# Four-tap filter of k as two passes in two 64-column tiles, with the moving operand stacked from two shifts

## Chip, cores, metric

The kernel runs on one core of a Trainium2 chip. The metric is the device time of one execution in microseconds. Each version was run several times. Every run is fast or slow (slow: over 1.5% above the fastest run of the same kernel), and only fast runs are compared. One execution of each version was traced, and all stage times below come from these traces.

## The reference, cut to what matters

The network is a gated long convolution followed by a two-layer MLP, on 2048 tokens of 512 channels. The change touches the first step only: a causal filter of `k` over four tokens, one set of four weights for each channel, multiplied by `v`.

```python
ks = 4
k_pad = jnp.pad(k, ((0, 0), (ks - 1, 0), (0, 0)))
k_shift = jnp.zeros_like(k)
for t in range(ks):
    k_shift = k_shift + k_pad[:, t:t + S, :] * shift_k[:, ks - 1 - t][None, None, :]
kv = k_shift * v
# ... kv is convolved with ssm_k over all 2048 tokens (by FFT), plus kv * ssm_D,
#     gated by layernorm(q), added to q; then layernorm, relu MLP, residual
```

## The kernel before

`k` arrives transposed, channels on partitions, in four chunks of 512 tokens. A unit is one chunk of 128 channels, so there are 16 units. TensorE computes a unit with four accumulating matmuls against diagonal weights, each reading `k` one token earlier. VectorE then multiplies the result in PSUM by `v`.

```python
def taps(u):
    c, rg = divmod(u, DC)
    ps = psum.tile([P, CH], F32, tag="ps", name="pkv")
    for j in range(KS):
        nc.tensor.matmul(out=ps[:], lhsT=wdiag[:, rg, j, :],
                         rhs=kT[:, rg, CH * c + 16 - j:CH * c + CH + 16 - j],
                         start=(j == 0), stop=(j == KS - 1))
    return u, ps
# times_v(u, ps): VectorE, kvx[...] = ps * vT[...]
```

The units of chunks 1 to 3 are interleaved with `group_k`, the first stage of the long filter's transform: 64 small matmuls, whose four results ScalarE (three) and VectorE (one) copy out. All these tiles take turns in eight PSUM banks.

```python
for gb in range(8):
    for u in ((4, 5), (6,), (7, 8), (9,), (10, 11), (12,), (13, 14), (15,))[gb]:
        times_v(*taps(u))
    group_k(gb)
for pq in halves:          # dre, dim: eight small GpSimd products that read dsc ("dm_f" in the trace)
    ...
# ... to_rows: TensorE transposes kv; needs the product of the last unit
pl.pop("early")            # the memory of dsc, d0, kfl, kvx and others is given back,
pl.pop("vp")
slotB = pl.push("slotB")   # and kf is laid over it
kf = slotB.tile([P, 2, 256, 32], F32R, tag="B", name="kf")
```

GpSimd negates a sine table, `cn` ("c2n" in the trace), in eight slices. Before the change it does so early.

## Time and profile before

| what | before |
|---|---|
| time, median of four fast runs (220.4 over the first three) | 220.3 us |
| traced span | 218.7 us |
| loop of taps and groups (to the transposes of kv) | ends at 37.0 us |
| second transform stage starts to use products (first `psy` matmul) | 67.4 us |
| first matmul of the MLP | 125.6 us |

The last three rows are milestones: each is the start of the first matmul that writes a given tile. If a change alters only the loop, the later milestones move by the same amount.

### The profile page before, as it was taken

Reading aid. Unit: us, or ns where it says so; the run is one execution under the profiler, and the core shown is the slowest. Engines: PE = TensorE matmul, PEld = TensorE weight load, DVE = VectorE, ACT = ScalarE, POOL = GpSimd, SP = SyncE. Lnnn points to the kernel's source line nnn. Section 1 sums busy time; section 2 is a strip of 40 time slices with the busy share of each in tenths; the row PEclk is TensorE's granted clock in tenths of the full one; section 3 lists DMA queues with packets and bytes.
Section 4 is the critical chain, followed back from the end, with each engine's and each line's share of the span. In section 5 each row is a group of like instructions: output and inputs, shape, how many; then the busy total and the mean of one; then the engine's idle time right before and its main releaser. Section 6 shows DMA issues by size and latency. Waiting matters only on the chain.

```text
span 218.7 us, 7281 instructions
## 1 busy us (share of the span) xinstructions
PE 202.8 (93%) x3103; PEld 139.4 (64%) x3122; DVE 148.2 (68%) x304; ACT 127.7 (58%) x242; POOL 65.9 (30%) x99
## 2 busy tenths in 40 slices
PE   7879889999979999989987899999999999999993
PEld 2276446999968999879965587444444444444442
DVE  7978868899979999957968779742973257130032
ACT  2587858788867888858966699003740066206500
POOL 6059920000029999969200120210021002000000
PEclk9969999999999999999999999999999999999999
DMA  6999960000000000059970000332022110421012
GB/s 96 383 224 191 142 136 7 3 4 3 6 3 0 1 0 3 1 134 216 305 252 3 6 0 3 42 77 55 24 52 63 42 47 0 96 57 42 0 42 54
DMA packets 30383, 15.40 MB, mean 70 GB/s; under 512 B 25520, under 2 KB 29072, under 8 KB 30224
## 3 DMA queue, kind: packets, MB, share of 16 engines
q1 hardware_dynamic: 29520, 14.76, 29.9%
q8 instruction: 24, 0.39, 0.8%
q10 hardware_dynamic: 832, 0.20, 0.4%
q14 instruction: 7, 0.06, 0.1%
HBM read 7.08 MB, written 2.10 MB: 42 GB/s over the span
## 4 chain that ended last, share of the span: by engine, by line
PE 83%; ACT 6%; DMA 4%; issue 2%; DVE 2%; SPq 1%; ACTq 0%
PE ps2m L568 17%; PE ps1m L556 16%; PE pz L482 8%; PE psi L449 7%; PE psy L375 7%; PE pst L217 5%; PE ps L244 4%; PE pkv L271 4%; PE ps2k L259 4%; DMA pre<-in_A_ssm_k_dram 4%; PE ps2k L261 3%; PE u L259 3%; PE u L261 3%; ACT ecore L143 1%; SPq L121 1%
## 5 line engine op out<-in xcount | busy, mean ns | idle before, releaser
L556 PE MATMUL ps1m<-hlnT,w 128*128 128x512 bf16 (+3 forms) x219 | 39.5, 336 | 0.3
L558 ACT ACTIVATE h1T<-ps1m 128x512 bf16<-128x512 f32 (+3 forms) x55 | 27.4, 514 | 21.2 <-PE ps1m L556 20.3
L568 PE MATMUL ps2m<-w,h1T 128*128 128x512 bf16 (+3 forms) x177 | 38.9, 366 | 0.7 <-issue 0.3
L570 DVE TENSOR_TENSOR o<-ps2m,xh 128x512 bf16<-128x512 f32 (+1 forms) x17 | 11.1, 659 | 38.1 <-PE ps2m L568 37.6
L556 PEld LDWEIGHTS <-w 128*128 128x128 bf16 (+1 forms) x220 | 21.7, 100 | 17.6 <-issue 1.4
L568 PEld LDWEIGHTS <-h1T 128*128 128x128 bf16 (+1 forms) x187 | 17.6, 98 | 21.2 <-issue 3.1
L365 DVE TENSOR_TENSOR t<-u,kf 128x704 fp32r<-128x704 f32 x32 | 26.7, 887 | 2.9 <-ACT usb L361 2.6
L365 POOL TENSOR_TENSOR t<-usb,kf 128x320 fp32r<-128x320 f32 x32 | 28.1, 922 | 1.4 <-ACT usb L361 1.0
L493 ACT CAST zt<-pz 128x512 bf16<-128x512 f32 x16 | 8.4, 592 | 29.2 <-PE pz L482 29.2
L482 PE MATMUL pz<-bp,ecore 32*32 32x128 f32 x1024 | 22.5, 384 | 2.3 <-issue 1.4
L231 ACT CAST a<-ps 128x512 fp32r<-128x512 f32 (+1 forms) x42 | 21.2, 575 | 4.3 <-PE ps L244 4.2
L502 POOL TENSOR_SCALAR rstd<-mv 128x4 f32<-128x4 f32 (+1 forms) x7 | 1.6, 232 | 70.3 <-DVE mv L509 70.3
L482 PEld LDWEIGHTS pz<-bp,ecore 32*32 32x32 f32 x1024 | 14.2, 103 | 9.4 <-issue 5.4
L231 ACT CAST kf<-psy 128x512 fp32r<-128x512 f32 x30 | 17.4, 640 | 1.7 <-PE psy L375 0.2
L233 DVE CAST a<-ps 128x512 fp32r<-128x512 f32 (+1 forms) x26 | 16.1, 647 | 3.1 <-PE ps L244 2.9
L507 DVE BATCH_NORM_STATS2 st<-xh 128x6 f32<-128x512 bf16 x28 | 17.4, 680 | 0.0
L449 PE MATMUL psi<-dre,kf 128*128 128x256 f32 x64 | 15.5, 284 | 0.9 <-ACT kf L231 0.9
L375 PE MATMUL psy<-t,ipos 128*128 128x512 f32 x48 | 15.8, 391 | 0.0
L271 PE MATMUL pkv<-kT,wdiag 128*128 128x512 bf16 x56 | 14.8, 380 | 0.8 <-DMA kT<-in_A_k_dram 0.3
L449 PE MATMUL psi<-dim,kf 128*128 128x256 f32 x64 | 15.4, 283 | 0.0
L209 POOL TENSOR_SCALAR c2n<-c2s 128x512 fp32r<-128x512 f32 x8 | 11.9, 1559 | 8.9 <-ACT c2s L177 8.9
L449 PEld LDWEIGHTS psi<-dre,kf 128*128 128x128 f32 x64 | 12.3, 192 | 1.3 <-ACT kf L231 1.3
(115 smaller groups left out, 377.0 us busy)
## 6 DMA issues: line engine op xcount, KB each, us to landing
pre<-in_A_ssm_k_dram SPq DMA_DIRECT2D x1, 2048.0 KB, 8.7
out_dram<-o SPq DMA_DIRECT2D x58, 32.0 KB, 1.6
xh<-in_A_q_dram SPq DMA_DIRECT2D x4, 384.0 KB, 6.8
w<-in_B_w_dram SPq DMA_DIRECT2D x1, 1376.0 KB, 12.7
w<-in_B_w_dram SPq DMA_DIRECT2D x1, 1280.0 KB, 15.8
xh<-in_A_q_dram SPq DMA_DIRECT2D x4, 128.0 KB, 2.8
hlnT<-hln SPq DMA_TRANSPOSE x12, 2.4
w<-in_B_w_dram SPq DMA_DIRECT2D x1, 96.0 KB, 15.4
```

What stands on the lines that cost most here:

```text
L231: nc.scalar.copy(out=o, in_=i)
L233: nc.vector.tensor_copy(out=o, in_=i)
L259: nc.tensor.matmul(out=ps[:, kk, :], lhsT=w_re[:, k1, :], rhs=a_in(col(k1, 0)), start=True, stop=False, skip_group_check=True)
L271: nc.tensor.matmul(out=ps[:], lhsT=wdiag[:, rg, j, :], rhs=kT[:, rg, CH * c + 16 - j:CH * c + CH + 16 - j], start=(j == 0), stop=(j == KS ...
L365: eng.tensor_tensor(out=t[:, :, j, :], in0=in0.unsqueeze(1).to_broadcast([P, 2, n, 2]), in1=kfr[:, :, j, ks], op=ALU.mult)
L375: nc.tensor.matmul(out=psy[:], lhsT=m_[:], rhs=t_.rearrange("p j k -> p (j k)"), start=first, stop=not first)
L449: nc.tensor.matmul(out=ps[:, i, :], lhsT=kf[:, c, 4 * m:4 * m + 4, :].rearrange("p r k -> p (r k)"), rhs=d[:].rearrange("p a b -> p (a b)" ...
L482: nc.tensor.matmul(out=pz[32 * a:32 * a + 32, r4, l4, :], lhsT=ecore[rows, rho, n2, :], rhs=rhs, start=(rho == 0), stop=(rho == 1), tile_p ...
L507: nc.vector.bn_stats(out=st[:, t % 4, :], in_=xh[:, t, :])
L556: nc.tensor.matmul(out=ps1[:fsz, :], lhsT=w1[:, c, fc * P:fc * P + fsz], rhs=hlnTs[sc][:, c, part], start=(c == 0), stop=(c == DC - 1))
L558: nc.scalar.activation(out=h1s[sc][:fsz, fc, part], in_=ps1[:fsz, :], func=ACT.Relu)
L568: nc.tensor.matmul(out=ps2[:], lhsT=h1s[sc][:ksz, fc, i * P:(i + 1) * P], rhs=w2[:ksz, fc, ds], start=(fc == 0), stop=(fc == NFC - 1))
```

## The change

The intent is to halve TensorE's work on chunks 1 to 3. A diagonal weight matrix of 128 x 128 uses one row for each column. The change instead lets 128 rows hold 64 channels twice, once as they are and once two tokens later, so that one pass does two taps for 64 channels. The two halves of the channels sit in two tiles of 64 columns, which can run at the same time. The price is three VectorE copies for each chunk, which build the stacked operand. In the code, `lo` and `hi` are partitions 0 to 63 and 64 to 127.

```diff
     def taps(u):
         ...
-        for j in range(KS):
-            nc.tensor.matmul(out=ps[:], lhsT=wdiag[:, rg, j, :], rhs=kT[:, rg, ...],
-                             start=(j == 0), stop=(j == KS - 1))
+        if c == 0:
+            ...                       # as before
+        else:
+            for p in range(2):
+                for hf, (src, o) in enumerate(((kAs[c], 2), (kTs[c], 16))):
+                    nc.tensor.matmul(out=ps[halves[hf], :], lhsT=wd2[:, rg, hf, p, :],
+                                     rhs=src[:, rg, o - p:o - p + CH],
+                                     start=(p == 0), stop=(p == 1),
+                                     tile_position=(0, 64 * hf), skip_group_check=True)
+    def pair_up(c):
+        kA = kAs[c] = kvp.tile([P, DC, CH + 2], BF16, tag="kA", name="kA", bufs=2)
+        kc = kTs[c]
+        nc.vector.tensor_copy(out=kA[lo, :, :], in_=kc[lo, :, 14:16 + CH])
+        nc.vector.tensor_copy(out=kA[hi, :, :], in_=kc[lo, :, 12:14 + CH])
+        nc.vector.tensor_copy(out=kc[lo, :, 14:16 + CH], in_=kc[hi, :, 12:14 + CH])
 ...
+    pair_up(1)                        # after the transposes of the long filter
     for gb in range(8):
-        for u in ((4, 5), (6,), (7, 8), (9,), (10, 11), (12,), (13, 14), (15,))[gb]:
+        group_k(gb)
+        if gb == 2:
+            pair_up(2)
+        if gb == 4:
+            pair_up(3)
+        for u in ((4, 5), (6, 7), (8, 9), (10, 11), (12,), (13, 14), (15,), ())[gb]:
             times_v(*taps(u))
-        group_k(gb)
+        if gb == 4:                   # GpSimd's negated table, moved here from before the loop;
+            ...                       # its first write reads a result of pair_up(3), so that it waits
     for pq in halves:
         ...                           # dre and dim: unchanged text, now behind that table on GpSimd
 # ... also: k loaded into four tiles with 16 tokens of overlap; wq, wd2: the new weights, on VectorE
```

More of the change, by code (lines that the diff above doesn't have):

```diff
@@ L104 @@
     vTs = [vp.tile([P, DC, CH], BF16, name=f"vT{c}") for c in range(4)]
-    kT = kvp.tile([P, DC, 16 + S], BF16, name="kT")
+    kTs = [kvp.tile([P, DC, 16 + CH], BF16, name=f"kT{c}") for c in range(4)]
+    kAs = {}
+    wq = kvp.tile([P, DC, 2, 2], BF16, name="wq")
     wdiag = kvp.tile([P, DC, KS, P], BF16, name="wdiag")
@@ L113 @@
         nc.tensor.matmul(out=warm[:], lhsT=wz[:, 0:P], rhs=wz[:], start=True, stop=True)
-    nc.vector.memset(kT[:, :, 0:16], 0.0)
+    nc.vector.memset(kTs[0][:, :, 0:16], 0.0)
     for c, src in ((0, "k"), (0, "s"), (0, "v"), (1, "k"), (1, "v"), (2, "k"), (2, "v"), (3, "k"), (3, "v")):
@@ L120 @@
         elif src == "k":
-            nc.sync.dma_start_transpose(out=kT[:, :, 16 + CH * c:16 + CH * c + CH], in_=k_d[ts, :])
+            if c == 0:
+                nc.sync.dma_start_transpose(out=kTs[0][:, :, 16:16 + CH], in_=k_d[ts, :])
+            else:
+                nc.sync.dma_start_transpose(out=kTs[c][:], in_=k_d[CH * c - 16:CH * c + CH, :])
         else:
@@ L168 @@
                                 in1=wsh[:, rg, :].unsqueeze(2).to_broadcast([P, KS, P]), op=ALU.mult)
+    id64 = early.tile([P, 64], BF16, name="id64")
+    nc.vector.tensor_tensor(out=id64[:], in0=ident[:, 0:64], in1=ident[:, 64:128], op=ALU.add)
+    wd2 = kvp.tile([P, DC, 2, 2, 64], BF16, name="wd2")
     cc = wp.tile([P, 32, P], F32R, name="c2c")
@@ L204 @@
     table(cc, r2[:], (0,))
-    dtab = consts.tile([P, 8, DC, 8], BF16, name="dtab")
-    for h in range(8):
-        hs = slice(4 * h, 4 * h + 4)
-        nc.gpsimd.tensor_single_scalar(out=cn[:, hs, :], in_=cs[:, hs, :].bitcast(F32), scalar=-1.0, op=ALU.mult)
-        if h == 0:
-            nc.gpsimd.tensor_copy(out=dtab[:], in_=d0[:].rearrange("p r (o g) -> p o r g", g=8))
+    for row in range(2):
+        for hf in range(2):
+            j0 = 0 if row == hf else 2
+            nc.vector.tensor_copy(out=wq[halves[row], :, hf, :], in_=wsh[halves[hf], :, j0:j0 + 2])
+    nc.vector.tensor_tensor(out=wd2[:].rearrange("p r h j i -> p (r h j) i"),
+                            in0=id64[:].unsqueeze(1).to_broadcast([P, 4 * DC, 64]),
+                            in1=wq[:].rearrange("p r h j -> p (r h j)").unsqueeze(2).to_broadcast([P, 4 * DC, 64]),
+                            op=ALU.mult)
     def to_rows(cols, q, fl, eng):
@@ L269, in taps @@
         ps = psum.tile([P, CH], F32, tag="ps", name="pkv")
-        for j in range(KS):
-            nc.tensor.matmul(out=ps[:], lhsT=wdiag[:, rg, j, :], rhs=kT[:, rg, CH * c + 16 - j:CH * c + CH + 16 - j],
-                             start=(j == 0), stop=(j == KS - 1))
-        return u, ps
+        if c == 0:
+            for j in range(KS):
+                nc.tensor.matmul(out=ps[:], lhsT=wdiag[:, rg, j, :], rhs=kTs[0][:, rg, 16 - j:16 - j + CH],
+                                 start=(j == 0), stop=(j == KS - 1))
+        else:
+            for p in range(2):
+                for hf, (src, o) in enumerate(((kAs[c], 2), (kTs[c], 16))):
+                    nc.tensor.matmul(out=ps[halves[hf], :], lhsT=wd2[:, rg, hf, p, :], rhs=src[:, rg, o - p:o - p + CH],
+                                     start=(p == 0), stop=(p == 1), tile_position=(0, 64 * hf), skip_group_check=True)
+        return u, ps
+    def pair_up(c):
[4 more added lines that the diff above has]
+        nc.vector.tensor_copy(out=kc[lo, :, 14:16 + CH], in_=kc[hi, :, 12:14 + CH])
     def times_v(u, ps):
@@ L306 @@
     for gb in range(8):
-        for u in ((4, 5), (6,), (7, 8), (9,), (10, 11), (12,), (13, 14), (15,))[gb]:
-            times_v(*taps(u))
-        group_k(gb)
+        group_k(gb)
[4 more added lines that the diff above has]
+        for u in ((4, 5), (6, 7), (8, 9), (10, 11), (12,), (13, 14), (15,), ())[gb]:
+            times_v(*taps(u))
+        if gb == 4:
+            dtab = consts.tile([P, 8, DC, 8], BF16, name="dtab")
+            nc.gpsimd.tensor_copy(out=dtab[lo, 0, 0, 0:1], in_=kTs[3][lo, 0, 14:15])
+            for h in range(8):
+                hs = slice(4 * h, 4 * h + 4)
+                nc.gpsimd.tensor_single_scalar(out=cn[:, hs, :], in_=cs[:, hs, :].bitcast(F32), scalar=-1.0, op=ALU.mult)
+                if h == 0:
+                    nc.gpsimd.tensor_copy(out=dtab[:], in_=d0[:].rearrange("p r (o g) -> p o r g", g=8))
     for pq in halves:
```

## The prediction

> **What bounds the kernel now.** I read the page's first two parts, then the chain of waits, to learn in which stage the changed instructions lie; then the busy time by stretch for that stage; then VectorE's own timeline there, because the change puts new work on that engine. The page says that TensorE is the engine to look at and that its clock dips only once, early:
>
> ```profile
> span 218.7 us, 7281 instructions
> PE 202.8 (93%) x3103; PEld 139.4 (64%) x3122; DVE 148.2 (68%) x304; ACT 127.7 (58%) x242; POOL 65.9 (30%) x99
> PEclk9969999999999999999999999999999999999999
> ```
>
> The share over the whole span is an average, so the stage decides. The chain of waits in order of time (start, duration, what; cut to 18 to 42 us) shows one unbroken alternation of tap matmuls (line L271) and first-stage matmuls of k (L244), all on TensorE, with two stretches of "issue":
>
> ```profile
> 22.39 0.66 PE ps L244 x61
> 23.04 0.32 PE pkv L271
> 23.42 1.46 PE pkv L271 x6
> 24.88 0.61 PE ps L244 x64
> ...
> 26.91 0.62 issue
> ...
> 31.63 0.73 issue
> ...
> 36.98 3.77 PE pst L217 x64
> ```
>
> So from 19 to 37 us TensorE sets the pace, and the taps carry it. The busy times by stretch (us; PE, PEld, DVE, ACT, POOL, granted clock, DMA share, GB/s) are the important view:
>
> ```profile
> 12.00:18.70 6.70, 6.41 (x65) 6.41 (x66) 5.49 (x10) 4.50 (x4) 5.27 (x5) 0.75 1.23 234
> 18.70:37.00 18.30, 16.12 (x554) 8.67 (x560) 13.85 (x22) 13.94 (x25) 10.17 (x15) 1.00 0.73 113
> 37.00:41.00 4.00, 4.00 (x68) 4.00 (x69) 3.86 (x7) 3.58 (x7) 0.00 (x0) 1.00 0.00 0
> ```
>
> In the middle row TensorE has 16.1 of 18.3 us, but VectorE and ScalarE are close behind with 13.9 each. If TensorE gets faster, the stage can shrink by some 4 us at most before another engine is full, and VectorE is the one that gets new work. Its timeline there (start, duration, idle before in brackets):
>
> ```profile
> 17.14 2.48 DVE L221 TENSOR_SCALAR kfl<-pst 128x512 int32<-128x512 int32 x4
> 20.39 1.29 DVE L278 TENSOR_TENSOR kvx<-pkv,vT 128x512 bf16<-128x512 f32 x2 [0.77 <-DMA vT<-in_A_v_dram]
> 27.97 0.69 DVE L233 CAST a<-ps 128x512 fp32r<-128x512 f32 x1 [0.78 <-PE ps L244]
> 32.09 0.69 DVE L278 TENSOR_TENSOR kvx<-pkv,vT 128x512 bf16<-128x512 f32 x1 [0.97 <-DMA vT<-in_A_v_dram]
> 36.23 0.69 DVE L278 TENSOR_TENSOR kvx<-pkv,vT 128x512 bf16<-128x512 f32 x1 [0.20 <-PE pkv L271]
> 37.66 3.97 DVE L221 TENSOR_SCALAR xfl<-pst 128x512 int32<-128x512 int32 x6
> ```
>
> The multiplication by v of the last tap unit ends at 36.92 us, and 0.06 us later the transposes of kv start on TensorE (36.98). From there on TensorE is busy to the end, so the time of the whole kernel moves with the end of that one VectorE instruction. That is the quantity I predict.
>
> **What the Trainium skill says.** "TensorEngine Tiling (Array Packing)", section Tiling Modes, says that tiles execute weight loads and matmuls independently and in parallel, and that changing the mode drains the engine. The trace before agrees on the first: the 256 matmuls per half of L244, in four row tiles, come four in some 0.03 us. The number of mode changes stays about the same, since taps (128 rows) and L244 (32 rows) already differ. "VectorE: DVE Perf Modes", section on the perf-mode tier table, gives 693 ns for a bf16 copy of 2048 elements within SBUF, its fastest mode; no such copy is in the trace before. "SBUF — State Buffer", section "SBUF: two separate sides", says that such a VectorE copy and a GpSimd instruction lock each other out for a whole instruction; the change moves the negated sine table (GpSimd) behind the last copy, so I expect no clash. "TensorE: Matmul & The Clock Gate", Part 1, says that TensorE falls to half clock after about a 3.4 us window of little work. The trace has the case: idle from about 10.2 to 12.3 us, then clock 0.50 to 16 us.
>
> **The change part by part.**
> TensorE: chunks 1 to 3 have 12 tap units of 4 matmuls over 512 columns. A unit pair takes from 22.98 to 24.81 us, 1.83 us, so a unit costs about 0.9 us and a matmul about 0.21. Now a unit is two passes of two concurrent tiles, about 0.43 us. That removes 12 x 0.43 = 5.1 us from TensorE. What is left there: 12 x 0.43 + 8 x 0.65 (L244) + 1.4 of issue = 11.8 us.
> ScalarE: 24 casts at 0.52 us pitch (three take 1.56) = 12.5 us, unchanged.
> VectorE, old work: 8 casts and 12 multiplications; back to back such instructions come every 0.61 us (four of L221 in 2.48 us, each 0.69). 20 x 0.61 = 12.2 us.
> VectorE, new work: nine copies, three for each chunk, of 64 partitions x 4 x 514 = 2056 bf16. From the row of L46 (64 elements 196 ns, 2048 elements 1228 ns, int32, so 0.52 ns an element and 163 ns fixed) and half of that slope for bf16, one costs 163 + 2056 x 0.26 = 698 ns, in accord with the skill's 693. With some overlap of neighbours I take 0.68 each: 2.05 us per chunk and 6.15 in all. There are also four small weight copies (about 0.15 each), the new weight table of 1024 elements (L167 takes 688 ns for 512, at one element a cycle another 512 are 0.53: 1.22 us) and the 64-column identity (0.2).
>
> Where it lies. The weight table comes after the cosine turns end at 12.24 us. VectorE is idle there for 1.03 us until the first transposes arrive, so about 0.9 of its 2.0 us delay the evictions of kfl: their end moves from 19.62 to about 20.5. TensorE's first-stage group 0 needs all of them, and starts at about the old time (20.6 against 20.42), because the taps that stood before it are now behind it. Then VectorE, in program order, has three copies, group 0's cast, two multiplications and so on, to the last multiplication: 6.15 + 19 x 0.61 = 17.7 us. Twice, for chunks 2 and 3, the next VectorE instruction is the multiplication whose taps wait for the copies just made: two passes, their latency and the signal back, about 0.7 us of idle each. For chunk 1 a cast lies between.
> Sum: 20.5 + 17.7 + 1.4 = 39.6 us, against 36.92 before: +2.7 us. VectorE takes TensorE's place as the bound, and the 5.1 us gained become TensorE waiting.
> GpSimd: the table is 8 x 1.48 us pitch (7 in 10.34) and starts near 35.5 us; its first slice is there at 37, the first use is after 43, and a slice is used every 2.7 us. It stays off the path. The transposing loads grow by 3% (528 rows for 512); k's chunk 3 is issued at 22.3 and lands some 5.6 us later, well before its copies at about 33.
>
> **The rivals.**
> (a) VectorE absorbs the copies. For it: VectorE idles about 4.3 us between 19.62 and 36.92 (17.3 us less 20 instructions at about 0.65). Against it: the new work is 6.15 in the loop plus 0.9 before it. At a pitch of 0.55 for a copy, without the two waits, the end is about 37.1 us: no change, 220.5. A gain of over 4.4 us needs VectorE's work to vanish, which I cannot see.
> (b) The copies do not run in the fastest mode, because of their 64 partitions, four rows or crossing of partitions. At half rate a copy is 163 + 1070 = 1.23 us, nine are 11.1: another 4.9 us, about 228. Everything is even and aligned, so I hold it unlikely.
> (c) The clock. While copies for a chunk run, TensorE has about 2.8 us without work, more than the idle stretch that cost it its clock at 13 us. One or two cold windows of 3.4 us double some 2 us of work each: +1 to +3 us, above all if one falls into the 3.8 us of transposes. I add 0.3 to the middle for it and widen the range upwards.
> (d) The two column tiles do not overlap. TensorE then has 17 us as before beside VectorE's 19: still VectorE-bound, with waits of 1.1 in place of 0.7 us, about 224.
>
> **Range and chances.** 220.4 + 2.7 + 0.3 = 223.4; rival (a) pulls down, so I take 223.1. From (a) without waits (220.5) to (c) with two cold windows (226) is my 8 in 10. Slower by over 2% means above 224.8: it needs (b), (c) or (d) on top, 0.21. Faster by over 2% means below 216.0: 0.03. The rest, 0.76, is within 2%.
>
> **What would show it right or wrong.** Right: VectorE over 90% busy from about 20 to 40 us; nine copies near 0.7 us; TensorE's matmuls there waiting for VectorE; idle VectorE of about 0.7 us after the copies of chunks 2 and 3; the transposes of kv starting near 39.6 us and everything after them the same length. Wrong: transposes starting before 37 us (copies cheaper or hidden), copies at 1.2 us, or a granted clock of 0.5 in slices between 20 and 45 us.

## More of the kernel before

GpSimd matters later, so here are two lines of its timeline in the kernel before (start, duration, instruction). They show that the table is done at 25.6 us and that the last of the small products that read `dm_f` is done at 29.1 us:

```profile
15.27 10.34 POOL L209 TENSOR_SCALAR c2n<-c2s 128x512 fp32r<-128x512 f32 x7
...
28.32 0.80 POOL L312 TENSOR_SCALAR dim<-dm_f 64x64 fp32r<-64x64 f32 x2
```

## The result, and the profile after

The change made the kernel slower. Its four fast runs took 230.46 to 232.91 us, median 231.77, against 220.31 for the kernel before. The ratio is 1.0506, with a 95% interval of 1.0427 to 1.0585. A ratio here is the mean time of one kernel's fast runs over that of the other's of the same rounds, so it is not quite the ratio of the quoted medians. The traced run of the changed kernel is the slowest of its four (232.91 us), so the two traced spans lie 12.4 us apart where the medians lie 11.5 apart.

The head of the page of the changed kernel. In the last line, each digit is the granted clock of one of 40 slices in tenths; slices 4 to 7 (17 to 40 us) and 10 (52 to 58 us) have fallen from 9, and slice 3 was low before too:

```profile
span 231.1 us, 7304 instructions
PE 206.5 (89%) x3111; PEld 141.3 (61%) x3122; DVE 155.6 (67%) x319; ACT 127.5 (55%) x242; POOL 66.0 (29%) x100
PEclk9977677997999999999999999999999999999999
```

The busy times by stretch, with the same columns as in the prediction (us; PE, PEld, DVE, ACT, POOL, clock, DMA share, GB/s):

```profile
18.70:37.00 18.30, 12.24 (x355) 6.37 (x353) 14.95 (x24) 10.67 (x18) 0.00 (x0) 0.72 0.79 116
37.00:41.00 4.00, 3.04 (x72) 1.49 (x74) 2.52 (x4) 0.71 (x3) 2.53 (x4) 0.61 0.02 4
49.00:51.00 2.00, 1.28 (x70) 1.03 (x68) 0.00 (x0) 0.00 (x0) 2.00 (x3) 1.00 0.03 8
51.00:53.00 2.00, 0.00 (x0) 0.00 (x0) 0.00 (x0) 0.00 (x0) 1.81 (x7) 1.00 0.00 0
```

Two things stand out. From 18.7 to 37 us no engine is full (VectorE, the fullest, has 14.95 of 18.3 us), although the stage is longer than before, and the clock is 0.72 instead of 1.00. From 51 to 53 us only GpSimd works.

The milestones put sizes on them:

| milestone | before | after | moved by |
|---|---|---|---|
| transposes of kv start | 37.0 | 43.9 | 6.9 |
| first `psy` matmul | 67.4 | 80.0 | 12.6, so 5.7 more |
| first matmul of the MLP | 125.6 | 138.0 | 12.4 |
| end of the span | 218.7 | 231.1 | 12.4 |

So there are two losses: 6.9 us in the loop, and 5.7 us between the transposes and the first product. Nothing after that changed.

VectorE's timeline of the changed kernel (start, duration, idle time before in brackets) answers the one in the prediction:

```profile
17.69 2.48 DVE L233 TENSOR_SCALAR kfl<-pst 128x512 int32<-128x512 int32 x4
...
28.57 0.68 DVE L298 COPY kA<-kT 64x2056 bf16<-64x2056 bf16 x1
29.26 0.69 DVE L299 COPY kA<-kT 64x2056 bf16<-64x2056 bf16 x1
29.98 0.69 DVE L300 COPY kT<-kT 64x2056 bf16<-64x2056 bf16 x1
31.46 0.69 DVE L305 TENSOR_TENSOR kvx<-pkv,vT 128x512 bf16<-128x512 f32 x1 [0.79 <-PE pkv L289]
...
39.42 0.69 DVE L305 TENSOR_TENSOR kvx<-pkv,vT 128x512 bf16<-128x512 f32 x1 [1.10 <-PE pkv L289]
...
44.68 3.90 DVE L233 TENSOR_SCALAR xfl<-pst 128x512 int32<-128x512 int32 x6
53.79 1.29 DVE L371 TENSOR_TENSOR kf<-ps2k,dtab 128x512 fp32r<-128x512 f32 x2 [5.22 <-POOL dim L353]
```

The copies take 0.69 us each, as predicted. But between 20 and 44 us VectorE idles 4.9 us in thirteen gaps (the sum of the bracketed times of its instructions there), all of them waits for TensorE. The prediction had 1.4. The last line is the second loss: the first write into `kf` waits 5.2 us for GpSimd. GpSimd's own timeline says what it did until then:

```profile
38.38 0.18 POOL L345 COPY dtab<-kT 64x1 bf16<-64x1 bf16 x1 [33.32 <-DVE kT L300]
...
40.48 10.24 POOL L348 TENSOR_SCALAR c2n<-c2s 128x512 fp32r<-128x512 f32 x7
...
52.96 0.80 POOL L353 TENSOR_SCALAR dim<-dm_f 64x64 fp32r<-64x64 f32 x2
```

The table starts at 38.4 us, because its first write was made to wait for the last copy. The small products that read `dm_f` come behind it in GpSimd's order, and the last ends at 53.8 us. At that moment `kf` is written for the first time. In the kernel before they were done at 29.1 us. `kf` uses none of their results, but it is laid over the memory in which `dm_f` lay. Not all of the 5.7 us is waiting: TensorE stands still for 4.25 us until `kf` is written, and then its clock is 0.50 from 55.0 to 58.4 us.

TensorE's waits inside the loop are these (the changed kernel's timeline of TensorE, two tap matmuls after the copies for chunk 2; then the granted clock of single microseconds, in the columns used above):

```profile
30.00 0.40 PE L289 MATMUL pkv<-kA,wd 128*64 128x512 bf16 x1 [2.15 <-DVE kA L299]
30.73 0.38 PE L289 MATMUL pkv<-kT,wd 128*64 128x512 bf16 x1 [0.32 <-DVE kT L300]
```
```profile
30.00:31.00 1.00, 0.68 (x5) 0.30 (x7) 0.67 (x1) 0.00 (x0) 0.00 (x0) 1.00 1.06 236
32.00:33.00 1.00, 1.00 (x61) 0.80 (x64) 0.84 (x2) 0.00 (x0) 0.00 (x0) 0.50 0.00 0
```

TensorE idles 2.15 us, starts again at full clock, and about 1 us later its clock is halved for some 3 us. The loop has three such stretches: at clock 0.50 TensorE runs from about 20.8 to 27.7, 31.1 to 34.5 and 37.9 to 41.3 us. In these stretches VectorE waits for slow matmuls. The last two follow waits for copies, of 2.15 and 2.17 us. The first and longest begins before TensorE has waited for any copy: it follows a wait of 1.42 us for `kfl` before group 0, where the kernel before has taps to do. So it comes, at least in its beginning, from the new order and not from the copies.

The changes of the clock lie on a grid. Here they fall at 20.8, 27.7, 31.1, 34.5, 37.9, 41.3, 55.0 and 58.4 us, all a multiple of 3.41 us apart, and the halved stretches of every trace of this case last 3.4, 6.8 or 10.2 us (but for one cut off by the end of a trace). The grid lies elsewhere in each run (in pool_early below, 34.8 and 41.6 us), so whether a given wait costs clock is partly chance.

### The profile page after: what moved, and what is told of

Its sections match the earlier page's. It is cut to its first block, busy times and chain, and to the rows that moved or that the text cites. A ratio compares the mean times of both kernels' runs of the same rounds, so it can differ in the third digit from the quotient of the medians.

```text
span 231.1 us, 7304 instructions
## 1 busy us (share of the span) xinstructions
PE 206.5 (89%) x3111; PEld 141.3 (61%) x3122; DVE 155.6 (67%) x319; ACT 127.5 (55%) x242; POOL 66.0 (29%) x100
## 4 chain that ended last, share of the span: by engine, by line
PE 58%; DVE 10%; POOL 3%; ACT 2%; issue 2%; SPq 1%; DMA 1%; DVEq 0%; ACTq 0%
PE ps2m L609 13%; PE ps1m L597 12%; PE psi L490 6%; PE psy L416 6%; PE pz L523 5%; PE ps2k L271 4%; DVE st L548 4%; PE ps2k L273 3%; PE u L271 3%; PE u L273 3%; PE ps L256 2%; POOL rstd L544 2%; SPq L614 1%; DVE hln L554 1%; DVE qln L554 1%
## 5 line engine op out<-in xcount | busy, mean ns | idle before, releaser
L490 PE MATMUL psi<-dre,kf 128*128 128x256 f32 x64 | 15.5, 284 | 0.9 <-ACT kf L243 0.9
L372 ACT CAST kf<-ps2k 128x512 fp32r<-128x512 f32 x16 | 10.6, 669 | 9.1 <-POOL dim L353 5.9
L289 PE MATMUL pkv<-kA,wd 128*64 128x512 bf16 x24 | 10.5, 550 | 4.8 <-DVE kA L299 4.8
L371 DVE TENSOR_TENSOR kf<-ps2k,dtab 128x512 fp32r<-128x512 f32 x16 | 10.4, 684 | 5.5 <-POOL dim L353 5.2
```

What stands on the lines that cost most here:

```text
L490: nc.tensor.matmul(out=ps[:, i, :], lhsT=kf[:, c, 4 * m:4 * m + 4, :].rearrange("p r k -> p (r k)"), rhs=d[:].rearrange("p a b -> p (a b)" ...
```

## The experiments

Two theories were to be told apart for each loss. For the loop: VectorE's time for the copies (the predicted mechanism), or TensorE's halved clock. For the stall: reuse of memory behind the last small product, or a need for the table itself. The table collects all results; "transposes" is the first milestone, "psy" the second.

| run | time, median of fast runs (us) | ratio to before, 95% interval | transposes | psy minus transposes |
|---|---|---|---|---|
| before | 220.3 | 1 | 37.0 | 30.4 |
| after | 231.8 | 1.0506, 1.0427 to 1.0585 | 43.9 | 36.1 |
| pool_early | 224.4 | 1.0152, 1.0061 to 1.0244 | 42.5 | 30.4 |
| cn_back | 228.0 | 1.0322, 1.0242 to 1.0402 | 45.6 | 30.5 |
| warm | 225.8 | 1.0187, 1.0112 to 1.0261 | 40.7 | 30.3 |
| no_copies (wrong result) | 222.5 | 1.0042, 0.9970 to 1.0114 | 38.7 | 30.4 |
| copies_only | 225.4 | 1.0234, 1.0189 to 1.0279 | 42.0 | 30.6 |
| no_copies_warm (wrong result) | 222.8 | 1.0111, 1.0061 to 1.0162 | 37.5 | 30.4 |
| two_chunks | 222.2 | 1.0092, 1.0053 to 1.0131 | 38.3 | 30.4 |
| one_chunk | 221.5 | 1.0045, 0.9999 to 1.0091 | 37.0 | 30.4 |
| order_only | 222.5 | 1.0083, 1.0037 to 1.0130 | 39.2 | 30.4 |
| free_old_order (wrong result) | 222.6 | 1.0115, 1.0066 to 1.0164 | 37.9 | 30.4 |

Below the row "after", the first four runs shared one set of runs of the kernel before (median 221.06), the next four another (220.16), the last two a third (220.28). The sets ran on different chips, so between sets the ratios are compared. One run each of pool_early, no_copies and one_chunk was slow and is left out. The milestones come from a single trace of each, and where the clock falls differs from run to run, so differences under about 1 us between them say little. The traced run of cn_back is the slowest of its four (230.46 us; the others 227.70 to 228.14), and those of no_copies_warm, two_chunks and one_chunk are the fastest of theirs, 0.9 to 1.8 us under the medians. All versions from warm on, but for two_chunks and one_chunk, have the change of pool_early in them. The three kernels that compute wrong taps still passed the comparison with the reference, so that comparison cannot vouch for the taps of any version.

### pool_early: the small products moved ahead of the table

```diff
     nc.gpsimd.memset(dim[:].bitcast(F32), 0.0)
+    for pq in halves:
+        ...                           # the eight products into dre and dim
     ...
-    for pq in halves:
-        ...
```

> The changed kernel, but GpSimd builds dre and dim (eight small products that read dm_f) before the loop instead of after the negated sine table. Theory (reuse of memory): the first eviction into kf waits for GpSimd's last reader of the memory that kf takes over, which was the dim product; with that early, the first kf eviction starts some 0.5 us after its matmuls (near 48.5 us instead of 53.8), the stall of 3.5 us and the cold clock behind it (55 to 58 us) go, and the time falls by 5 to 6 us to about 226. Rival (kf waits for all of GpSimd's table, or for the slices of it): the stall only shortens to the end of the table near 50.7 us, and the time falls by 2 to 3 us to about 229. The loop before it stays as it is: transposes of kv start near 44 us in both.

The time fell from 231.8 to 224.4 us. The distance from transposes to psy went back to 30.4 us, the value of the kernel before, so the whole second loss is gone. VectorE's and GpSimd's timelines of this run show that it was not the table:

```profile
47.08 1.43 DVE L371 TENSOR_TENSOR kf<-ps2k,dtab 128x512 fp32r<-128x512 f32 x2
```
```profile
37.89 10.24 POOL L351 TENSOR_SCALAR c2n<-c2s 128x512 fp32r<-128x512 f32 x7
```

`kf` is written at 47.08 us without a wait on VectorE's side, while GpSimd is still busy with the table until 48.1. The rival (the end of the table) predicted a remaining stall, and there is none. What the products themselves cost in their new place is visible too: at 7 to 15 us, beside VectorE's integer arithmetic above all, a pair of them took 1.6 to 2.1 us instead of 0.7 to 0.8. Four of the eight ended 0.21 to 0.23 us after the end of a VectorE instruction that ran beside them. That fits the lock that the Trainium skill describes in "SBUF — State Buffer", section "SBUF: two separate sides".

### cn_back: the table back in its old place

```diff
-        if gb == 4:
-            ...                       # the table, waiting for pair_up(3)
+    dtab = ...; for h in range(8): ...   # the table, before the loop, as in the kernel before
```

> The changed kernel with the negated sine table on GpSimd where it was before the change (13 to 26 us). The stall at kf must go in any theory, so about 226 from that alone. If VectorE's fast copies and GpSimd's table lock each other out, the three copies of chunk 1 (near 20 to 22 us) take 1 to 1.5 us each instead of 0.69, or wait, and the transposes of kv start 1 to 3 us later than in pool_early; if they do not, the copies stay at 0.69 us and the time equals pool_early within 0.5 us.

The stall is gone here too (30.5). The copies of chunk 1 now fall beside the table, and VectorE's timeline, with one slice of the table from GpSimd's, shows what that costs:

```profile
21.58 1.00 DVE L305 COPY kA<-kT 64x2056 bf16<-64x2056 bf16 x1
22.62 0.98 DVE L306 COPY kT<-kT 64x2056 bf16<-64x2056 bf16 x1
```
```profile
22.01 2.05 POOL L228 TENSOR_SCALAR c2n<-c2s 128x512 fp32r<-128x512 f32 x1
```

Two of the three copies take about 1.0 us instead of 0.69, and the set is longer by 0.6 us. The slice of the table takes 2.05 us instead of 1.48. So the two do slow each other, and moving the table away from the copies had a reason. But the second copy shown runs from start to end inside that slice, so neither was locked out for a whole instruction of the other. The collision explains only a small part of the 3.1 us by which the transposes start later than in pool_early. In this trace, the slowest run of its four, TensorE ran 13.7 us of the loop at half clock against 6.8 there, and I did not separate the two further. Waiting with the table saved this collision and brought the 5.7 us stall.

### warm: the clock held up by extra matmuls

```diff
+    def keep_warm(n):                 # n matmuls on a tile of ones into a spare PSUM tile
+        ...
     for gb in range(8):
+        if gb == 0: keep_warm(6)
         group_k(gb)
+        if gb == 0: keep_warm(5)
         if gb == 2:
             pair_up(2)
+            keep_warm(12)
         if gb == 4:
             pair_up(3)
+            keep_warm(12)
```

> pool_early with 35 extra matmuls on ones, in the three places where TensorE waits for the copies (11 around group 0, 12 after each of pair_up 2 and 3). Theory (half clock): about 13 of the 23 us of the loop run at clock 0.5, and of VectorE's 4.9 us of idle time there some 3 us come from matmuls that take twice as long. With the clock held at 1.0 the transposes of kv start at 41 us (44 in pool_early) and the time falls by 2.5 to 3 us. Rival (VectorE's copies alone set the end): the clock is 1.0 and the start of the transposes stays within 0.7 us of pool_early.

The stretch table of this run shows the clock at 1.00 throughout the loop, and VectorE full in the second row:

```profile
18.70:37.00 18.30, 17.41 (x428) 8.75 (x431) 15.89 (x27) 10.77 (x18) 0.72 (x2) 1.00 0.84 125
37.00:41.00 4.00, 3.69 (x207) 2.37 (x191) 3.99 (x7) 3.43 (x7) 4.00 (x4) 1.00 0.02 4
```

VectorE's idle time in the loop falls to 2.3 us, 0.68 of it after the copies of chunk 2 and 0.68 after those of chunk 3, and the transposes start at 40.7 us: 3.2 earlier than in the changed kernel, which had 13.7 us of its loop at half clock, and 1.8 earlier than in pool_early, which had 6.8 (34.8 to 41.6 us). That is the halved clock's share. The rest, 3.7 us against the kernel before, remains with the clock at 1.00. The time did not fall below pool_early (225.8 and 224.4, intervals overlapping). In the trace of warm the clock was halved later, near 120 to 130 us in a stage that the change doesn't touch, and the way from the first `psi` matmul to the MLP took 31.8 us instead of 30.1. So the expected gain showed at the milestone, not in the total.

### no_copies, no_copies_warm, free_old_order: what would the tiles be worth if the copies were free?

All three compute wrong taps: both tiles read the loaded `k`, and no copies are made. no_copies keeps the changed kernel's order. no_copies_warm adds 15 extra matmuls to hold the clock. free_old_order goes back to the old order of taps and groups.

```diff
-        nc.vector.tensor_copy(...)    # the three copies of pair_up
+        kAs[c] = kTs[c]               # all three kernels
+        if gb == 0: keep_warm(9)      # no_copies_warm only, before group 0
+        if gb < 3: keep_warm(2)       # no_copies_warm only, after groups 0 to 2
```

> Wrong result on purpose: pool_early without the nine copies; both column tiles read the k tile as it was loaded, everything else (two passes, two tiles, same sizes) is kept. It shows what the taps in column tiles are worth if the copies were free. If the tiles run concurrently and the copies are the whole cost, VectorE and ScalarE set the pace (12.2 and 12.5 us of work) and the transposes of kv start at 34.5 to 35.5 us, 1.5 to 2.5 us earlier than in the kernel before, at clock 1.0; time about 218.5. If the tiles or the mode switches cost more than thought, they start at 36.5 us or later, about 220.5.

> Wrong result on purpose: no_copies with 15 extra matmuls on ones where TensorE waits (nine before group 0, two after each of groups 0 to 2), so that the clock stays at 1.0. no_copies started the transposes at 38.7 us with the clock at 0.5 from 21.8 to 28.8 us. If the half clock is all that kept the free-copy case from winning, the transposes now start at 35 to 36.5 us, before the 37.0 of the kernel before, and the time is about 219.5. If something else sets the end (ScalarE's casts from 21.9 us at 1.56 us a group, the load of v's last chunk near 32 us, the taps behind group 0), it stays at 37 us or later, 220.5 or more.

> Wrong result on purpose: column tiles without copies as in no_copies, but in the old order of taps and groups, so that TensorE has the taps of units 4 and 5 to do while VectorE evicts kfl. It is the ceiling of the idea. If instruction fetch (gaps of 0.6 to 1.8 us called issue, one per 256 TensorE instructions) and the load of v's last chunk near 32 us set the end, the transposes start at 36 to 37.5 us, about 220; if they do not, TensorE's 11.8 us and ScalarE's 12.5 us of work let them start at 34.5 to 35.5 us, about 218.5.

None of them beats the kernel before. The transposes start at 38.7, 37.5 and 37.9 us. In no_copies and free_old_order the clock was 0.50 for about seven microseconds of the loop, but in no_copies_warm it was 1.00 all the time. Its chain of waits (start, duration, what) shows what took the place of the tap matmuls:

```profile
21.35 0.32 PE idle L301
...
22.87 0.49 PE ps L256 x49
23.36 1.83 issue
25.19 0.29 PE ps L256 x15
...
32.50 0.70 issue
...
34.73 0.62 PE ps L256 x64
35.34 0.55 PE pkv L289 x4
35.90 0.34 PE ps L256 x5
36.24 0.69 issue
```

The taps are as cheap as hoped: four pairs of column-tile matmuls take 0.99 us elsewhere in the same chain, so a pair takes 0.25 us and a unit 0.50, where a unit took 0.9 before. But three stretches of "issue", 3.2 us together, stand where TensorE waits for nothing that the profile shows. They fall in a pattern. Count TensorE's instructions from the start of the program, each matmul with its weight load as two. The first gap comes after 22 (first warm-up) + 32 (chunk 0) + 128 (transposes) + 18 (nine extra) + 128 (group 0) + 4 (two extra) + 16 (units 4 and 5) + 98 (49 of group 1) = 446. The same count gives 958 and 1214 for the other two, and 702 and 958 for the two gaps of the kernel before that the prediction shows. All of these are 190 plus a multiple of 256. The page's table of queues for this run has one for instructions:

```profile
q8 instruction: 24, 0.39, 0.8%
```

Its 0.39 MB in 24 packets are 16 KB each. "Advanced Engine Details and Errata" of the Trainium skill, section ISA Cache, gives a cache line of 16 KB, or 256 instructions. So these look like waits for the next block of instructions. At the same count of 446, the wait was not visible in the kernel before, 0.51 us in pool_early, 1.83 here and 2.12 in free_old_order, at a time when k and v were being loaded. That it depends on those loads was not tested.

The experiment has a handicap of its own: the pairs of extra matmuls after groups 0 to 2 ("idle" in the lines) stand in the same chain, 0.47 us each time (0.32 in the line shown, and 0.15 of "issue" behind it), 1.4 us together. Without them, and with the clock still at 1.00, the loop might have ended somewhat earlier than before; no run shows that.

The load of v sets another bound, which no form of the taps moves. In the kernel before, the multiplication of the first unit of chunk 3 waits 0.97 us for it and starts at 32.09 us, and five more VectorE instructions follow up to the end of the last multiplication. At 0.61 us each that is 35.8 us instead of 36.9, so an estimate of the most that the loop could gain with the loads as they are is about 1 us.

So with the copies free, no run ended the loop earlier than before, and by this estimate the most to be had was about 1 us.

### copies_only and order_only: the costs without the tiles

Both keep the old taps in all chunks and the changed kernel's order; both give right results. copies_only makes the nine copies into a tile that nobody reads. order_only makes none.

```diff
-            for p in range(2): ...    # column tiles
+            for j in range(KS):       # the old four matmuls, on kTs[c]
+                nc.tensor.matmul(out=ps[:], lhsT=wdiag[:, rg, j, :], ...)
-        # the three copies of pair_up: kept in copies_only (all into kA), removed in order_only
```

> pool_early with the old taps (four matmuls with 128x128 weights for every chunk), while VectorE still makes all nine copies in the same places, now into a tile that nothing reads; right result. If the copies cost by VectorE's time alone, its work from 20.4 us is 6.2 of copies and 11.6 of the rest plus a little idle, so the transposes of kv start at 38.5 to 40.5 us (37.0 in the kernel before, 40.7 in warm), at clock 1.0 because TensorE no longer waits for copies; time 222 to 224. If the cost of the change lies in the wait of the taps for the copies rather than in VectorE's time, the start is within 0.8 us of 37.0 and the time near 220.5.

> copies_only without the copies: the old taps in the changed kernel's order (group 0 before any tap of chunk 1, two units after each early group), weight table still built, dre and dim early; right result. It separates the order from the copies: copies_only started the transposes of kv at 42.0 us. If the copies are what costs there, this starts at 37 to 38.5 us and takes 220.5 to 222 us, so the copies cost 3.5 to 5 us. If the new order costs most of it (TensorE idle before group 0, then half clock), the start is at 39.5 us or later and the time 223 or more.

order_only starts the transposes at 39.2 us and takes 222.5 us; copies_only starts them at 42.0 and takes 225.4. The copies therefore cost 2.8 us of the loop and 2.9 us of time even when no matmul waits for them (ratios 1.0234 and 1.0083, from two sets of runs). The changed order and the weight table cost another 2.2 us. Part of that is again a halved clock, from 21.5 to 24.9 us, after TensorE had waited 1.46 us before group 0 (the kernel before has taps to do there). My expectation for order_only, 37 to 38.5, was too low, and the clock expected of copies_only too high (two halved stretches instead of none). The copies of chunk 3 took 0.91 to 0.98 us in copies_only, because the table no longer waited for them and ran beside them; that is 0.8 us of the 2.8. And one of the two halved stretches, from 39.2 to 42.6 us, is missing in order_only.

The comparison that matters most: copies_only, without any column tile, and pool_early, which has them, cannot be told apart (ratios 1.0234 and 1.0152 with overlapping intervals; transposes at 42.0 and 42.5 us). If the tiles return anything of what their preparation costs, it does not show here.

### two_chunks and one_chunk: attempts to keep the idea

In two_chunks, chunk 1 uses the old taps, chunks 2 and 3 the tiles, and the copies are made one at a time between other VectorE work, before they are needed. The weight table moves to GpSimd, and the negated table goes back to its old place. one_chunk does this for chunk 3 alone.

```diff
+    PLAN = ((4, 5, "g"), (6, (2, 0), "g", (2, 1)), ((2, 2), 7, 8, "g"), (9, "g", (3, 0)),
+            (10, (3, 1), 11, (3, 2), "g"), (12, "g"), (13, 14, "g"), (15, "g"))
+    # a number: the taps of that unit; (c, i): copy i of chunk c; "g": group_k
```

> An attempt to keep the idea: chunk 1 on the old taps (so TensorE has taps before group 0 as in the kernel before), chunks 2 and 3 in column tiles with the copies made one at a time between other VectorE work and one or more steps before the taps that need them; the weight table on GpSimd between slices of the negated sine table, which is back at its old place. VectorE has 12.2 + 4.1 = 16.3 us of work from 19.6 us, so the transposes start at 36.5 to 38 us; TensorE never waits 2 us, clock 1.0. Time 220 to 222. If copies and GpSimd collide (0.7 to 1.0 us more in all), 0.5 us later.

> As two_chunks with only chunk 3 in column tiles. VectorE has 12.2 + 2.05 = 14.3 us from 19.6, TensorE 1.7 us less than before. v's last chunk lands near 32 us and six VectorE instructions of 0.61 us follow up to the last multiplication, so the transposes start at 36 us at best, 37 at worst; time 219.5 to 220.5, within 1% of the kernel before.

Most of the loss is gone. two_chunks takes 222.2 us (transposes at 38.3) and one_chunk 221.5 (37.0, the same as before). Neither is faster than the kernel before, although both were traced in their fastest runs, and the interval of two_chunks excludes equality. No version tried beats the kernel before, and none of the experiments points to one.

## Why the prediction was wrong

The prediction was 223.1 us with a range up to 226.0; the result is 231.8. Its direction and the path that it named were right. Two terms of its sum were wrong: 0.3 us for the halved clock, which cost 3.2, and nothing for GpSimd, which cost 5.7.

**The bound and the quantity to watch: right.** The prediction tied the time to the start of the transposes of kv. From there to the end the kernel before takes 181.7 us (218.7 - 37.0), and pool_early 182.1 (224.6 - 42.5). The changed kernel takes 187.2, and the excess is the stall. But VectorE was not over 90% busy from 20 to 40 us, as its list of signs asked (15.5 of 20 us), and the sign of being wrong that it named, a clock of 0.5 between 20 and 45 us, was there.

**The new VectorE work: right.** Copies 0.69 us each (predicted 0.68 to 0.70), 2.03 to 2.1 us a chunk (2.05), weight table 1.23 (1.22), the four small copies 0.69 in all (0.6), kfl done at 20.2 us (20.5). Rival (b), slow copies, is out. Rival (d), tiles that don't overlap, is out too: the matmuls that run side by side in the two tiles start within 0.06 us of each other, and a pair takes 0.25 us. A unit takes 0.50 us where 0.43 was predicted, because the old matmul was read as 0.21 us when 1.83 us for eight are 0.23; TensorE was not the bound, so this did not matter.

**"about 0.7 us of idle each", 1.4 us in all, and "I add 0.3 to the middle" for the clock: the first right as far as it went, the second wrong.** The two waits that it named measured 0.79 and 1.10 us, and 0.68 each with the clock held (warm). But VectorE idled 4.9 us in thirteen gaps; the other eleven, 3.05 us, lie in the stretches of halved clock or at their ends. The prediction saw the cause and named it as rival (c): 2.8 us without work for TensorE, "more than the idle stretch that cost it its clock at 13 us". It then entered it with 0.3 us. It was worth 3.2 us (43.9 against 40.7) in this trace, and 1.8 by pool_early's. The evidence for taking it seriously had been read, and the average of a risk was put where the likely case belonged. The mechanism was right for the waits for copies, though the first halved stretch began with another wait, and the size was off by a factor of six to eleven.

With the clock held, the loop ends 3.7 us later than before, against 2.7 predicted for that part. The prediction took the new order of groups and taps as free; order_only shows that it is not (2.2 us, a part of it again clock), because TensorE has no taps to do while VectorE finishes kfl.

**"It stays off the path" (GpSimd): wrong, 5.7 us.** The prediction followed the table from its start to its first use, and that was right: the table was never waited for. It did not ask what stands behind the table in GpSimd's order. The eight products moved from 29 to 54 us without a line of theirs being changed, and the write into `kf` depends on them through memory that changes hands. pool_early removed exactly this and nothing else.

The sum of the traces: 6.9 us in the loop and 5.7 us of stall, less 0.2 us later, make the 12.4 us between the two spans. Of the 6.9 in the loop, 3.2 go with the halved clock and 3.7 with the copies and the order.

**"The 5.1 us gained become TensorE waiting": right, for more reasons than it gave.** It had VectorE alone in mind. In the three runs without copies nothing was gained either: stretches of "issue", waits between the engines, a halved clock in two of them and extra matmuls in the third filled the place. How much of that is instruction fetch stays open.

## What to carry to other kernels

When an instruction is moved later on an engine, list what stands behind it in that engine's order, and for each of these what waits for it, through reuse of memory as well as through data. Work taken from a busy engine is worth what the next engine leaves free, and here the preparation of the cheaper form used the engine that was next in line. Treat a wait of some 2 us on TensorE as a likely halved clock for the following few microseconds, not as a small risk.

## What the Trainium skill lacked or had wrong

- "TensorE: Matmul & The Clock Gate", section "Why this matters for your kernels", asks for no idle gaps above about 3 us. Shorter ones were enough here: after a wait of 2.15 us the clock was 0.50 for about 3 us (31.1 to 34.5), and in order_only a wait of 1.46 us before group 0 was followed by the same. It is not certain for every gap: in pool_early a wait of 2.33 us left the clock at 1.00, and the wait before the transposes of the long filter, at 10 to 13 us, was followed by half clock in the kernel before (2.08 us) and not in copies_only (2.79). Its Part 1 says that the window runs freely, which fits the grid of 3.41 us on which the clock changed; how much work in a window keeps the clock up was not worked out.
- "Advanced Engine Details and Errata", section ISA Cache, gives 256 instructions to a line but no cost of passing into the next; "Runtime: NRT & Kernel Launch", section "Instruction fetch mechanics", calls that cost mostly hidden. If the gaps at counts 256 apart are that, it was not always hidden: some passings showed no gap, others one of up to 2.12 us.
- "TensorEngine Tiling (Array Packing)" has no measured rate for two 64-column tiles. Here a pair with 512 columns takes 0.25 us at full clock, against 0.23 for one 128-column matmul before (1.83 us for eight), switches included.
- "SBUF — State Buffer", section "SBUF: two separate sides", says that of VectorE and GpSimd whoever starts first holds the ports for the whole instruction and the other is blocked. GpSimd's products fit that (0.8 to 1.1 us on average instead of 0.35 to 0.40). The copies beside the table do not: one ran from 22.62 to 23.60 us inside a table slice from 22.01 to 24.06 us, and took 0.98 us instead of 0.69, so both went on, more slowly. (The profile's spans on GpSimd are rough.)
- None of the pages cited here says that the first write into a reused stretch of memory waits for the last reader of what lay there before, so that an instruction can gate another whose data it never touches. It cost 5.7 us here.
